# First half step of a fused attention and FFN kernel: its product in two stages, another order of issue, and products of zeros at four places

## The chip, the cores and the metric

The kernel runs on one core of one Trainium2 chip. The metric is the device time of one execution in microseconds, median of three runs. Engines are named as the trace names them: PE is TensorE (products), PEld its weight loads, DVE is VectorE, ACT is ScalarE, POOL is GpSimd, SP is SyncE, which here issues all transfers.

## The reference

Chunked attention with 8 memory keys (4 batches, 8 heads, 768 positions, head size 64), and behind it a two-layer network on the 3072x512 result, in float32:

```python
for c in range(S // 32):
    k_full = concat(mem_k, k[:, :, max(0, 32*c - 16) : 32*c + 32 + 8])   # v_full likewise
    scores = q_c @ k_full.T / sqrt(64)
    a = exp(scores - max(scores)); a = a / (sum(a) + 1e-09)
    out[:, :, c] = a @ v_full
x = out as 3072 x 512
h = x @ w_in                                    # 512 -> 2048
g = where(h >= 1, h, where(h <= -1, 0, (h + 1)**2 / 4))
return g @ w_out                                # 2048 -> 512
```

## The kernel before

The 3072 tokens are cut into 6 blocks of 512. A block's attention gives `xth` and `xtl`, the rounded high part of x and the rest; every large product is made of three: high by high, high by low, low by high. For each of 16 slices `fc` of the hidden width, a **hidden step** (`ps_h`) makes 12 products of x with a slice of `w_in`, ACT and DVE turn them into `gw`, `gh`, `gl`, and an **output step** (`ps_o`) makes 12 products with a slice of `w_out`, added up in two pairs of banks `a0`, `a1` over all 16 slices.

The weights come packed: 16 packets `w0` to `w15`, two slices each. A packet is decoded by one ACT scaling, three DVE steps on `f`, an ACT cast to `wr` and a DVE subtraction for the low part (`decode`).

Blocks 0 and 1 are written as generators that a hand-laid table, `FIRST`, advances one step per name; each engine runs its instructions in the order in which the steps are issued:

- `g0` to `g3`, `first_attention`: the first block's attention in four groups (two halves of the tokens by two pairs of heads). Steps: scores on PE (`ps_s`), maximum on DVE (`mx`), subtraction (`pr`), exponential on ACT, sum (`den`), its +1e-9, reciprocal (`rin`), division (`pr`), four PE transposes into a `ps_h` bank, ACT's copy (`pt`), the values on PE (`ps_x`), ACT's cast `xth`, DVE's subtraction `xtl`.
- `n0` to `n3`, `attention`: the halves of the next two blocks in the same steps, with DVE transposes; scores and values share one pair of banks, `s`, so n1's scores wait until DVE has read n0's values for `xtl`.
- `A`, `B`, `J`, `C`, `D`, `E` with a slice number, `early_step`: a hidden and an output step. A and B take one half of block 0's tokens each (256 columns), J takes all; C, D, E are the same for block 1.
- `w`: `decode`. `+`: the next transfer of the list `early`, issued by SP; each later use of one of 8 transfer semaphores waits for the transfer before it.

From block 2 on a regular loop does a hidden step and the output step of two slices before. `PLACES` names the banks of each group: g0 `s`, g1 `a0`, g2 scores and values `a1`, g3 scores `a1`, values `s` (as pairs of scores and values: `("s","s")`, `("a0","a0")`, `("a1","a1")`, `("a1","s")`).

Ahead of everything, `keep_warm(8)` issues eight bf16 products of zeros, 512 columns wide, into a `ps_h` bank. All records of the profile carry line L63, the helper `InOrder` that keeps the program's order, so tiles' names are what tells them apart.

Of the kernel before, what the change touches and what calls it, by code (L numbers as in the profile page):

```python
# [28 lines left out]

FIRST = """
    + + g0 g0 + g0 g1 g0 + g0 g1 g1 g0 g0 + g1 g0 w0 g1 g0 + g1 g1 g1 g0 w0 g1 + w0 g2 g1 w0 g1 g2 +
    w0 g2 w1 g0 w0 + g2 w1 g1 g2 + g0 g2 g2 g2 + g0 g2 w1 g3 g2 g1 w1 + A0 w2 g3 w1 g3 A1 w2 + g3 w1
    w3 g3 g2 A0 g3 g3 + A1 g3 A2 w2 g2 w4 g3 g2 A2 A0 w2 g3 A0 + g3 w3 w2 A0 w3 A0 g3 g3 + w2 B0 A1
    w3 A3 A1 B0 + A1 w3 B0 B1 w4 B0 w3 A3 A1 + B1 B0 w4 w5 B2 B1 w6 A2 w4 n0 + A2 B1 A2 w4 B1 A2 A3
    w5 A3 B2 + A3 w5 B3 w8 B2 w7 B0 w4 + B2 w5 B3 A3 w9 B2 B3 B1 w6 B3 + w5 w6 J4 w10 B3 w5 + w6 w11
    B2 w7 J4 w7 J5 + w6 w7 w12 w6 + w7 B3 J4 J5 w8 J6 w7 + J4 J5 w13 J4 w9 J5 J4 J6 w9 + J5 w15 J6
    w9 J7 J6 w14 J6 n0 w9 J5 J7 w9 w8 J7 J8 w8 J7 J7 w8 w11 J6 w8 J8 w11 J8 J9 w10 J8 w10 w11 J7 J9
    J8 w10 w11 J9 n0 w10 J10 J9 w10 n0 J9 w12 J8 J10 w12 w12 J11 J10 w12 w11 J10 J10 w13 J9 J11 w12  # L40
    w13 w14 J12 J11 n0 J11 n0 n0 J10 n0 J12 J11 n0 n0 J13 n0 n0 n0 n0 J11 w13 J13 J12 w13 J13 w14
    J12 n0 J13 w13 J12 J14 + n0 w14 n0 n0 w14 J12 w14 J14 J13 J14 w15 J14 n1 w15 w15 J15 + n1 w15
    w15 J13 J15 n1 J15 n1 J14 C0 J15 n1 J14 n1 n1 C0 n1 n1 J15 C1 n1 n1 J15 n1 C1 n1 n1 C1 C0 C1 C2
    J15 J15 C0 C1 n1 J15 J15 C0 C2 C2 C0 + n1 C2 n1 n1 C3 C2 C1 C3 C3 D0 C3 C3 C2 D0 D0 D1 D0 D0 n2
    D1 D1 D2 D1 + n2 C3 D1 D2 n2 D0 D2 n2 D2 D3 n2 D2 D1 n2 n2 D3 n2 E4 D3 n2 D3 n2 n2 n2 D2 E4 D3
    n2 E5 n2 E4 E4 E4 D3 E5 E6 E5 E5 E5 E4 E6 E6 E6 n2 E6 E7 + n2 n2 n2 n3 E7 E5 + n3 n3 E7 E8 n3 E7
    n3 n3 n3 E6 n3 E8 n3 n3 n3 E9 n3 n3 n3 E8 n3 E7 E8 E9 E8 E7 + n3 E9 E9 n3 n3 E9 E10 E8 E10 E10
    E10 E11 E10 E9 E11 E11 E11 E12 E11 E10 E12 E12 E12 E13 E12 E11 E13 E13 E13 E14 E13 E12 E14 E14
    E14 E15 E14 E13 E15 E15 E15 E15
"""  # L50
# [18 lines left out]
def attn_ffn_kernel(ctx: ExitStack, tc: tile.TileContext, first_qk, first_v, qk, vw, w, out):  # L69
# [24 lines left out]
    def two_banks(tag, name):  # L94
        return ps_2.tile([P, 2, 512], F32, name=name, tag=tag)
# [116 lines left out]
    def first_attention(g):  # L212
        half, u = divmod(g, 2)
        c0 = half * NCH // 2
        src = qk_of[0, g].rearrange("p (r n) -> p r n", r=2)
        ps = two_banks(PLACES[g][0], "ps_s")[:, :, 0:HT]
        s = ps.rearrange("p h (r t w) -> p h r t w", r=2, w=W)
        for r in range(2):
            for c in range(NCH // 2):
                t, j = divmod(c, P // CHUNK)  # L220
                for h in range(2):
                    rows, k0 = slice(h * D, (h + 1) * D), HT + c * W
                    pe.matmul(
                        s[j * CHUNK : (j + 1) * CHUNK, h, r, t],
                        src[rows, r, c * CHUNK : (c + 1) * CHUNK],
                        src[rows, r, k0 : k0 + W],
                        start=True,
                        stop=True,
                    )
# [12 lines left out]
        dve.tensor_reduce(m3, s, axis=AX.X, op=ALU.max)
        yield
        p4 = pr.rearrange("p (h n) w -> p h n w", h=2)
        dve.tensor_tensor(p4, s, m3.unsqueeze(3).to_broadcast([P, 2, n, W]), op=ALU.subtract)
        yield
        act.activation(pr, pr, AF.Exp, scale=SCALE)
        yield
        yield from normalise(pr)

        ps = ps_h.tile([P, 512], F32, name="ps_h")
        for n in range(NG // 2):
            pe.transpose(ps[:, n * P : (n + 1) * P], pr[:, 2 * n : 2 * n + 2, :], ident)
# [198 lines left out]
    def early_step(name, blk, tokens, fc):  # L452
# [9 lines left out]
        wh, wl = weights(0, fc, 0), weights(0, fc, 1)  # L462
        terms = hidden_terms(wh, wl, xh, xl)
        for i, (m, x, cc) in enumerate(terms):
            pe.matmul(hp, m[:, cc * P : (cc + 1) * P], x[:, cc], start=i == 0, stop=i == len(terms) - 1)
        yield
        if n == 0:
# [236 lines left out]
```

## Time and profile before

| | us |
|---|---|
| median of 3 runs (608.12 to 608.40) | 608.17 |
| the profiled execution | 608.17 |
| its span in the profile | 606.4 |
| PE busy | 591.0 (97%) |
| DVE busy | 325.6 (54%) |
| ACT busy | 281.2 (46%) |

The span is what the profile shows from the first to the last instruction; the rest of an execution's time lies around it. The page's strips cut the span into 40 equal slices of 15.2 us; PEclk is the granted TensorE clock in tenths of 2.4 GHz. In the rows further down a time is in us from the span's start.

### The profile page before, as it was taken

Reading aid. Unit: us, or ns where it says so; the run is one execution under the profiler, and the core shown is the slowest. Engines: PE = TensorE matmul, PEld = TensorE weight load, DVE = VectorE, ACT = ScalarE, POOL = GpSimd, SP = SyncE. Lnnn points to the kernel's source line nnn. Section 1 sums busy time; section 2 is a strip of 40 time slices with the busy share of each in tenths; the row PEclk is TensorE's granted clock in tenths of the full one; section 3 lists DMA queues with packets and bytes.
Section 4 is the critical chain, followed back from the end, with each engine's and each line's share of the span. In section 5 each row is a group of like instructions: output and inputs, shape, how many; then the busy total and the mean of one; then the engine's idle time right before and its main releaser. Section 6 shows DMA issues by size and latency. Waiting matters only on the chain.

```text
span 606.4 us, 12265 instructions
## 1 busy us (share of the span) xinstructions
PE 591.0 (97%) x5496; PEld 483.7 (80%) x5496; DVE 325.6 (54%) x466; ACT 281.2 (46%) x503; POOL 0.7 (0%) x6
## 2 busy tenths in 40 slices
PE   5889999999999999999999999999999999999996
PEld 2888888888888888888888888888888888888885
DVE  5999999987483224736424734623553632322222
ACT  2689764544444434344434434434433343533342
POOL 0000000000000000000000000000000000000000
PEclk8699999999999999999999999999999999999999
DMA  8999200433131004012201213101310000100001
GB/s 353 423 418 420 124 1 1 175 110 137 31 145 70 1 0 175 30 42 105 70 1 73 103 70 106 70 1 54 121 70 2 1 2 0 70 0 1 0 1 69
DMA packets 9845, 55.31 MB, mean 91 GB/s; under 512 B 1089, under 2 KB 1089, under 8 KB 5185
## 3 DMA queue, kind: packets, MB, share of 16 engines
q1 hardware_dynamic: 9792, 54.53, 23.2%
q8 instruction: 43, 0.70, 0.5%
q14 instruction: 10, 0.07, 0.0%
HBM read 48.23 MB, written 6.29 MB: 90 GB/s over the span
## 4 chain that ended last, share of the span: by engine, by line
PE 94%; DVE 3%; ACT 1%; DMA 1%; issue 0%; DVEq 0%; ACTq 0%
PE ps_o L63 44%; PE ps_h L63 44%; PE ps_x L63 3%; PE ps_s L63 3%; DVE f L63 1%; DMA qk<-in_first_qk_dram 1%; DVE pr L63 1%; DVE mx L63 0%; DVE den L63 0%; ACT w L63 0%; ACT gw L63 0%; DVE wr L63 0%; DVE xtl L63 0%; ACT pr L63 0%; ACT wr L63 0%
## 5 line engine op out<-in xcount | busy, mean ns | idle before, releaser
L63 PE MATMUL ps_o<-wr,gh 128*128 128x512 f32 x768 | 199.5, 396 | 0.0
L63 PE MATMUL ps_h<-xth,wr 128*128 128x512 f32 (+1 forms) x832 | 197.3, 379 | 0.0
L63 PEld LDWEIGHTS ps_h<-xth,wr 128*128 128x128 f32 x832 | 148.7, 189 | 31.9 <-DVE wr L63 0.5
L63 PEld LDWEIGHTS ps_o<-wr,gh 128*128 128x128 f32 x768 | 143.7, 188 | 32.5
L63 DVE SCALAR_TENSOR_TENSOR gw<-gw,gt 128x512 f32<-128x512 f32 (+1 forms) x104 | 67.2, 648 | 170.0 <-ACT gw L63 169.5
L63 ACT ACTIVATE gw<-ps_h 128x512 f32<-128x512 f32 (+1 forms) x104 | 58.7, 564 | 167.8 <-PE ps_h L63 167.7
L63 PE MATMUL ps_o<-wr,gl 128*128 128x512 f32 x384 | 109.0, 394 | 0.0
L63 PE MATMUL ps_h<-xtl,wr 128*128 128x512 f32 (+1 forms) x416 | 105.2, 375 | 0.0
L63 DVE TENSOR_TENSOR gl<-gw,gh 128x512 fp32r<-128x512 f32 (+1 forms) x104 | 67.4, 649 | 67.4 <-ACT gh L63 67.3
L63 ACT CAST gh<-gw 128x512 fp32r<-128x512 f32 (+1 forms) x104 | 61.1, 590 | 68.7 <-DVE gw L63 68.7
L63 PEld LDWEIGHTS ps_h<-xtl,wr 128*128 128x128 f32 x416 | 75.3, 190 | 14.1
L63 PEld LDWEIGHTS ps_o<-wr,gl 128*128 128x128 f32 x384 | 72.5, 189 | 17.2
L63 ACT ACTIVATE gw<-gw 128x512 f32<-128x512 f32 (+1 forms) x104 | 62.5, 601 | 0.0
L63 ACT ACTIVATE gt<-ps_h 128x512 f32<-128x512 f32 (+1 forms) x104 | 58.2, 559 | 0.0
L63 DVE STREAM_TRANSPOSE pt<-pr 32x512 f32<-32x512 f32 (+1 forms) x60 | 41.2, 698 | 1.3
L63 DVE SCALAR_TENSOR_TENSOR f<-w,f 128x1024 uint32<-128x1024 uint32 x32 | 38.9, 1220 | 0.4
L63 PEld LDWEIGHTS ps_x<-pt,v 64*64 64x64 f32 x1536 | 25.2, 142 | 5.5 <-issue 3.5
L63 ACT ACTIVATE pr<-pr 128x1024 f32<-128x1024 f32 (+1 forms) x14 | 13.1, 937 | 35.5 <-DVE pr L63 35.4
L63 PE MATMUL ps_x<-pt,v 64*64 64x32 f32 x1536 | 26.7, 226 | 1.6 <-ACT pt L63 1.6
L63 ACT CAST xth<-ps_x 128x512 fp32r<-128x512 f32 x24 | 13.1, 590 | 21.6 <-PE ps_x L63 21.5
L63 PEld LDWEIGHTS ps_s<-qk 64*32 64x32 f32 x1536 | 16.7, 110 | 6.4 <-issue 3.2
L63 ACT CAST wr<-f 128x1024 fp32r<-128x1024 f32 x16 | 16.8, 1050 | 9.3 <-DVE f L63 9.3
(27 smaller groups left out, 182.1 us busy)
## 6 DMA issues: line engine op xcount, KB each, us to landing
w<-in_w_dram SPq DMA_DIRECT2D x16, 1024.0 KB, 19.8
qk<-in_qk_dram SPq DMA_DIRECT2D x10, 1536.0 KB, 6.7
v<-in_vw_dram SPq DMA_DIRECT2D x10, 1024.0 KB, 5.1
out_dram<-ob SPq DMA_DIRECT2D x24, 256.0 KB, 2.0
qk<-in_first_qk_dram SPq DMA_DIRECT2D x4, 768.0 KB, 8.8
v<-in_first_v_dram SPq DMA_DIRECT2D x4, 512.0 KB, 12.8
```

The costliest lines, as they stand in the source:

```text
L63: return self.tc.keep_in_program_order(getattr(self.engine, name)(*args, **kwargs))
```

## The change

The table `FIRST` is replaced by another that advances the same generators in another order. Three things are new beside it:

- A name such as `z40x128` in the table calls `keep_warm(40, 128)`: 40 bf16 products of zeros, 128 columns wide, each with its weight load. There are four: 7 of 256 columns between the scores of g0 and g1, 40 of 128 behind g1's scores, 6 of 256 behind g0's transposes, 4 of 256 behind g1's.
- `keep_warm` writes into a bank of its own, `spare` (`ps_w`, in the pair `a1`), until g2's scores are issued, and `warm` is a constant tile.
- The step named by `APART`, A0, issues its 12 products in two stages: the eight with `xth`, a return to the table, and then the four with `xtl`.

The diff, with the table cut to its first lines:

```diff
 FIRST = """
-    + + g0 g0 + g0 g1 g0 + g0 g1 g1 g0 g0 + g1 g0 w0 g1 g0 + g1 g1 g1 g0 w0 g1 + w0 g2 g1 w0 g1 g2 +
-    w0 g2 w1 g0 w0 + g2 w1 g1 g2 + g0 g2 g2 g2 + g0 g2 w1 g3 g2 g1 w1 + A0 w2 g3 w1 g3 A1 w2 + g3 w1
+    + + g0 z7x256 g0 + g0 g1 z40x128 g0 + g0 g1 g0 g0 g1 + g0 g1 w0 g1 g0 z6x256 + g1 g1 g1 g0 w0 g1
+    z4x256 + w0 g2 g1 w0 g0 g2 + w0 g2 w1 g1 w0 + g2 w1 g0 g2 + g1 g0 A0 g2 g2 + g1 g2 g3 w1 A0 g3 +
...
 """
+
+APART = "A0"
...
         ps = two_banks(PLACES[g][0], "ps_s")[:, :, 0:HT]
+        if g == 2:
+            both["s2"] = True
...
         for i, (m, x, cc) in enumerate(terms):
+            if name == APART and i == 2 * NP:
+                yield
             pe.matmul(hp, m[:, cc * P : (cc + 1) * P], x[:, cc], start=i == 0, stop=i == len(terms) - 1)
...
-    def keep_warm(n):
-
-        ps = ps_h.tile([P, 512], F32, name="ps_h")
+    def keep_warm(n, cols):
+
+        ps = ps_h.tile([P, 512], F32, name="ps_h") if "s2" in both else spare
         for _ in range(n):
-            pe.matmul(ps, warm[:, 0:P], warm, start=True, stop=True)
+            pe.matmul(ps[:, 0:cols], warm[:, 0:P], warm[:, 0:cols], start=True, stop=True)
...
-    warm = gpool.tile([P, DM], BF16, name="warm", tag="gw")
+    warm = const.tile([P, DM], BF16, name="warm")
+    spare = two_banks("a1", "ps_w")[:, 0]
     dve.memset(warm, 0.0)
-    keep_warm(8)
+    keep_warm(8, DM)
...
+        if name[0] == "z":
+            keep_warm(*map(int, name[1:].split("x")))
+            continue
```

What it moves is read from the order of the built programs. First PE, from g2's scores (`qk_2`) to the first hidden steps (`wr_280` before and `wr_337` after are packet w0's decoded slices, the other one in these rows w1's; `pr_274` and `pr_331` hold g2's and g3's probabilities). Before:

```order
L63 MATMUL ps_s<-qk_2_189 32x64 x32
L63 MATMUL ps_x<-pt_127,v_130 64x32 x64
L63 MATMUL ps_h<-ident,pr_274 128x128 x4
L63 MATMUL ps_s<-qk_3_278 32x64 x32
L63 MATMUL ps_h<-xth,wr_280 128x256 x8
L63 MATMUL ps_h<-xtl,wr_280 128x256 x4
```

After:

```order
L66 MATMUL ps_s<-qk_2_242 32x64 x32
L66 MATMUL ps_x<-pt_134,v_137 64x32 x64
L66 MATMUL ps_h<-xth,wr_337 128x256 x8
L66 MATMUL ps_s<-qk_3_335 32x64 x32
L66 MATMUL ps_h<-xtl,wr_337 128x256 x4
L66 MATMUL ps_h<-ident,pr_331 128x128 x4
```

A0's eight products with `xth` now stand ahead of g3's scores, its four with `xtl` behind them, and g2's transposes come last.

Then DVE in the same place, from the sum of g2 (`f` of `w_203` or `w_260` is packet w1). Before:

```order
L63 TENSOR_REDUCE den<-pr_274 128x8
L63 TENSOR_SCALAR den<-den 128x8
L63 RECIPROCAL rin<-den 128x8
L63 TENSOR_TENSOR pr_274<-pr_274,rin 128x512
L63 TENSOR_TENSOR xtl<-ps_x,xth 128x2x256
L63 SCALAR_TENSOR_TENSOR f<-w_203,f 128x1024
L63 TENSOR_TENSOR xtl<-ps_x,xth 128x2x256
L63 SCALAR_TENSOR_TENSOR f<-w_203,f 128x1024
L63 TENSOR_REDUCE mx<-ps_s 128x8
```

After:

```order
L66 TENSOR_REDUCE den<-pr_331 128x8
L66 TENSOR_TENSOR xtl<-ps_x,xth 128x2x256
L66 TENSOR_SCALAR den<-den 128x8
L66 RECIPROCAL rin<-den 128x8
L66 TENSOR_TENSOR xtl<-ps_x,xth 128x2x256
L66 TENSOR_TENSOR pr_331<-pr_331,rin 128x512
L66 SCALAR_TENSOR_TENSOR f<-w_260,f 128x1024
L66 TENSOR_REDUCE mx<-ps_s 128x8
L66 TENSOR_TENSOR pr_331<-ps_s,mx 128x512
```

Both `xtl` moved ahead of g2's division, and one of the two steps of w1 moved behind g3's maximum.

Third, PE from n0's values (`ps_x<-pt,v`) to n1's scores (`ps_s<-qk`). Before:

```order
L63 MATMUL ps_x<-pt,v 64x32 x64
L63 MATMUL ps_h<-xth,wr_1220 128x512 x8
L63 MATMUL ps_h<-xtl,wr_1220 128x512 x4
L63 MATMUL ps_o<-wr_1220,gh 128x512 x8
L63 MATMUL ps_o<-wr_1220,gl 128x512 x4
L63 MATMUL ps_s<-qk 32x64 x64
L63 MATMUL ps_h<-xth,wr_1315 128x512 x8
```

After:

```order
L66 MATMUL ps_h<-xth,wr_1251 128x512 x8
L66 MATMUL ps_h<-xtl,wr_1251 128x512 x4
L66 MATMUL ps_x<-pt,v 64x32 x64
L66 MATMUL ps_o<-wr_1251,gh 128x512 x8
L66 MATMUL ps_o<-wr_1251,gl 128x512 x4
L66 MATMUL ps_s<-qk 32x64 x64
L66 MATMUL ps_h<-xth,wr_1394 128x512 x8
```

The hidden step that stood between the values and the scores now stands ahead of the values.

Last, DVE around the two `xtl` of n0. Before:

```order
L63 STREAM_TRANSPOSE pt<-pr 32x512 x4
L63 SCALAR_TENSOR_TENSOR f<-w_847,f 128x1024
L63 SCALAR_TENSOR_TENSOR gw<-gw,gt 128x512 x2
L63 SCALAR_TENSOR_TENSOR f<-w_854,f 128x1024
L63 TENSOR_TENSOR wr_1220<-f,wr_1220 128x1024
L63 TENSOR_TENSOR gl<-gw,gh 128x512
L63 SCALAR_TENSOR_TENSOR f<-w_854,f 128x1024
L63 TENSOR_TENSOR xtl<-ps_x,xth 128x4x2x64 x2
```

After:

```order
L66 STREAM_TRANSPOSE pt<-pr 32x512 x3
L66 TENSOR_SCALAR f<-w_951 128x1024
L66 SCALAR_TENSOR_TENSOR gw<-gw,gt 128x512
L66 TENSOR_SCALAR f<-w_939 128x1024
L66 SCALAR_TENSOR_TENSOR f<-w_939,f 128x1024
L66 TENSOR_TENSOR gl<-gw,gh 128x512
L66 SCALAR_TENSOR_TENSOR f<-w_939,f 128x1024
L66 TENSOR_TENSOR xtl<-ps_x,xth 128x4x2x64 x2
```

The first step of packet 15 (`w_951`) moved ahead of these `xtl`; over the whole stretch from packet w0's first step to them DVE has 125 instructions before and 127 after, the other one being a `gl`.

## Rows read from the trace of the kernel before

**Rows 1.** Stretches: length, each engine's busy us (instructions), clock, DMA share, GB/s.
```profile
0.00:111.90 111.90, 101.15 (x1176) 82.73 (x1176) 104.02 (x143) 74.15 (x122) 0.70 (x6) 0.92 0.60 245
...
111.90:601.76 489.86, 489.85 (x4321) 401.01 (x4320) 220.52 (x322) 206.66 (x380) 0.00 (x0) 1.00 0.15 55
...
13.42:109.94 96.52, 92.59 (x1028) 78.06 (x1029) 95.55 (x127) 68.79 (x116) 0.00 (x0) 0.93 0.57 236
```

**Rows 2.** Waits of PE: waiting line, waited for, us in total, times, longest.
```profile
PE ps_h L63 <- DVE pr L63: 6.6, 3, 4.1
```

**Rows 3.** Stretches of one us, columns as in rows 1: the clock.
```profile
9.00:10.00 1.00, 0.00 (x0) 0.00 (x0) 0.93 (x3) 0.00 (x0) 0.00 (x0) 0.58 1.00 422
...
18.00:19.00 1.00, 1.00 (x50) 1.00 (x44) 1.00 (x2) 1.00 (x2) 0.00 (x0) 0.50 1.00 408
...
26.00:27.00 1.00, 1.00 (x10) 1.00 (x9) 1.00 (x3) 1.00 (x2) 0.00 (x0) 0.89 1.07 434
```

**Rows 4.** Timeline of PE and PEld: start, us, engine, operation, count, idle before.
```profile
1.59 0.15 PEld L63 LDWEIGHTS <-warm 128*128 128x128 bf16 x1 [0.28 <-issue]
...
6.89 0.86 PE L63 MATMUL ps_s<-qk 64*32 64x64 f32 x64 [0.83 <-DMA qk<-in_first_qk_dram]
11.88 1.09 PE L63 MATMUL ps_h<-ident,pr 128*128 128x128 f32 x4 [4.13 <-DVE pr L63]
...
15.08 1.19 PE L63 MATMUL ps_s<-qk 64*32 64x64 f32 x64 [0.35 <-DMA qk<-in_first_qk_dram]
16.20 3.64 PE L63 MATMUL ps_x<-pt,v 64*64 64x32 f32 x128
...
23.72 2.08 PE L63 MATMUL ps_h<-xth,wr 128*128 128x256 f32 x8
...
26.36 1.11 PE L63 MATMUL ps_h<-xth,wr 128*128 128x256 f32 x8
...
29.05 1.22 PE L63 MATMUL ps_h<-xth,wr 128*128 128x256 f32 x8
...
30.59 0.60 PE L63 MATMUL ps_h<-ident,pr 128*128 128x128 f32 x4
32.77 1.14 PE L63 MATMUL ps_x<-pt,v 64*64 64x32 f32 x64 [1.58 <-ACT pt L63]
33.83 1.20 PE L63 MATMUL ps_o<-wr,gh 128*128 128x512 f32 x4
```

**Rows 5.** Timeline of DVE: the divisions of g0 and g3, g2's maximum and sum, w1.
```profile
11.04 0.69 DVE L63 TENSOR_TENSOR pr<-pr,rin 128x512 f32<-128x512 f32 x1
...
16.54 0.68 DVE L63 TENSOR_REDUCE mx<-ps_s 128x8 f32<-128x512 f32 x1
...
19.60 0.68 DVE L63 TENSOR_REDUCE den<-pr 128x8 f32<-128x512 f32 x1
...
23.70 1.22 DVE L63 SCALAR_TENSOR_TENSOR f<-w,f 128x1024 uint32<-128x1024 uint32 x1
24.83 0.68 DVE L63 TENSOR_REDUCE mx<-ps_s 128x8 f32<-128x512 f32 x1
...
29.05 0.69 DVE L63 TENSOR_TENSOR pr<-pr,rin 128x512 f32<-128x512 f32 x1
```

**Rows 6.** Timeline of ACT: the two casts of g0 and g1, a packet's scaling, a cast `gh`.
```profile
19.24 1.25 ACT L63 CAST xth<-ps_x 128x512 fp32r<-128x512 f32 x2
...
30.22 1.18 ACT L63 ACTIVATE w<-w 128x1024 f32<-128x1024 f32 x1
...
32.56 0.46 ACT L63 CAST gh<-gw 128x256 fp32r<-128x256 f32 x1
```

**Rows 7.** Timeline of DVE ahead of n1's scores.
```profile
96.00 0.25 DVE L63 RECIPROCAL rin<-den 128x16 f32<-128x16 f32 x1
96.29 1.22 DVE L63 TENSOR_TENSOR pr<-pr,rin 128x1024 f32<-128x1024 f32 x1
...
108.65 1.28 DVE L63 TENSOR_TENSOR xtl<-ps_x,xth 128x512 fp32r<-128x512 f32 x2
```

More of the change, by code (lines that the diff above doesn't have):

```diff
@@ L32 @@
 FIRST = """
-    + + g0 g0 + g0 g1 g0 + g0 g1 g1 g0 g0 + g1 g0 w0 g1 g0 + g1 g1 g1 g0 w0 g1 + w0 g2 g1 w0 g1 g2 +
-    w0 g2 w1 g0 w0 + g2 w1 g1 g2 + g0 g2 g2 g2 + g0 g2 w1 g3 g2 g1 w1 + A0 w2 g3 w1 g3 A1 w2 + g3 w1
-    w3 g3 g2 A0 g3 g3 + A1 g3 A2 w2 g2 w4 g3 g2 A2 A0 w2 g3 A0 + g3 w3 w2 A0 w3 A0 g3 g3 + w2 B0 A1
-    w3 A3 A1 B0 + A1 w3 B0 B1 w4 B0 w3 A3 A1 + B1 B0 w4 w5 B2 B1 w6 A2 w4 n0 + A2 B1 A2 w4 B1 A2 A3
-    w5 A3 B2 + A3 w5 B3 w8 B2 w7 B0 w4 + B2 w5 B3 A3 w9 B2 B3 B1 w6 B3 + w5 w6 J4 w10 B3 w5 + w6 w11
@@ L38 @@
[L38 to L47, printed above, removed]
@@ L48 @@
-    E10 E11 E10 E9 E11 E11 E11 E12 E11 E10 E12 E12 E12 E13 E12 E11 E13 E13 E13 E14 E13 E12 E14 E14
-    E14 E15 E14 E13 E15 E15 E15 E15
+    + + g0 z7x256 g0 + g0 g1 z40x128 g0 + g0 g1 g0 g0 g1 + g0 g1 w0 g1 g0 z6x256 + g1 g1 g1 g0 w0 g1
+    z4x256 + w0 g2 g1 w0 g0 g2 + w0 g2 w1 g1 w0 + g2 w1 g0 g2 + g1 g0 A0 g2 g2 + g1 g2 g3 w1 A0 g3 +
+    g2 g3 A0 w1 g3 A1 g2 g3 w1 + g3 g3 g3 w2 g2 A0 w1 A1 g3 + g2 w2 A2 A0 g2 g3 A0 w4 w2 g3 A2 w2 A0
+    g3 + w3 g3 A2 B0 w2 A1 w3 A2 w3 A1 + n0 B0 w2 B1 B0 A1 + B0 w4 A1 w5 B0 w3 B1 B2 A2 + w3 w4 A3
@@ new lines @@
+    B2 B1 w3 B1 w6 B3 + B2 B1 A3 w4 A2 B3 A3 w5 w4 + B0 w5 A3 B2 J4 w7 w4 w8 + B2 w6 w9 A3 B3 B1 w6
+    B3 J4 + w5 J5 w10 B3 J4 w5 w6 + B2 J4 w5 w11 A3 J4 J5 + w7 w7 B3 w12 w7 J6 w6 + J5 w13 w6 J5 n0
+    w7 + J4 w14 J5 w7 J6 + J7 w8 w15 J6 w8 J6 J6 J5 J7 w8 w9 w8 J7 w9 J8 J7 w9 w8 w9 J6 J8 J7 w10 w9
+    J9 w10 w11 w10 J7 J9 n0 J8 n0 J9 w11 J9 J10 J8 J9 w10 J8 n0 J8 J10 w10 n0 n0 w12 J10 J11 w11 J10
+    n0 w11 J10 J9 J11 w11 w12 J12 J11 w13 J11 w12 J11 w12 J10 w13 J12 w12 J12 J13 w13 J12 J12 w13 n0
@@ new lines @@
+    n0 J11 J13 n0 w13 n0 J14 n0 n0 w15 J13 n0 w14 J13 w14 J14 J13 J12 + n0 w14 n0 n0 w14 w14 n1 J14
+    J15 w15 J14 + J14 w15 J13 n1 w15 J15 n1 w15 C0 n1 J15 J14 n1 C0 J15 C0 n1 n1 C0 J15 n1 C1 C0 n1
+    J15 C1 n1 n1 n1 n1 C2 n1 C1 n1 J15 J15 C1 C2 C1 J15 J15 C2 C3 + n1 C2 n1 n1 C0 C3 C2 D0 C3 C3 C3
+    C1 D0 D0 D1 D0 D0 C2 D1 D1 D2 D1 D1 C3 D2 D2 D3 D2 D2 D0 D3 D3 E4 D3 D3 D1 E4 E5 E4 E4 E4 D2 E5
+    E6 E5 E5 E5 D3 n2 E6 E4 E6 + n2 E6 E6 n2 E7 n2 n2 E5 E7 n2 n2 n2 E7 E8 n2 E7 n2 E7 n2 n2 E6 E8
@@ L50 @@
+    n2 n2 E8 E8 n2 E8 E9 + n2 n2 n2 E7 E9 E9 E9 E10 E9 E8 E10 E10 E10 E11 E10 E9 E11 E11 E11 n3 E11
+    E10 + n3 n3 E12 n3 n3 n3 n3 E11 n3 E12 n3 n3 n3 E13 n3 n3 n3 E12 n3 E13 E12 E13 E14 + n3 E12 E13
+    n3 n3 E13 E12 E14 E14 E14 E15 E14 E13 E15 E15 E15 E15
 """
+APART = "A0"
 LAST = 2
```

## The prediction

> **What bounds the kernel now.** The table of stretches comes first: TensorE (PE) is busy for 101.15 of the first 111.90 us, idle for 10.75, and idle for 0.01 of the next 489.86 [rows 1], to 601.76, where only the last store is left. So after the first ramp the kernel is a queue of products without a gap, and a change in the ramp is worth as much as it brings that queue forward. TensorE's waits name the ramp's largest loss: 6.6 us behind VectorE's (DVE's) `pr` in three waits [rows 2]. The granted clock is the second loss: 0.58 in 9 to 10 us, 0.50 until it comes back in 26 to 27 [rows 3], that is 1.2 instead of 2.4 GHz, after TensorE had idled from 7.75 (6.89+0.86 [rows 4]). Third view: DVE is busy 95.55 of the 96.52 us from 13.42 to 109.94 [rows 1]. Through the ramp DVE, not TensorE, has no slack; TensorE can work ahead of it only as far as the order allows.
>
> The profiled execution took 608.17 us, its span 606.4; the 1.77 outside stay, and 608.17 is also the median of the runs shown. I call faster or slower what moves by over 0.2%, 1.22 us, about what a measurement of this kernel can tell from no change.
>
> **Where both orders meet.** The scores of n1 (64 products on `ps_s`, 111.90 before) are the place to compare at: behind them stand 3168 products in either program, the same number of each shape. Before, TensorE runs from there to 601.76 with no wait [rows 1]. If the order after has none there either, the end moves by as much as the start of these scores. That start is the later of two: TensorE's own arrival, and DVE's release, since the scores overwrite the bank from which n0's two `xtl` are still read.
>
> **The order's part: TensorE's arrival.** DVE's work is unmoved up to the sum `den` of g2 at 19.60 [rows 5]; g2's scores cannot start before their load, and started at 15.08 [rows 4]. From 19.60 I set each instruction in the new order behind its engine and its inputs, with the lengths of the rows. ACT's two casts `xth` run 19.24 to 20.49 [rows 6], so A0's first eight products start near 19.9 instead of 23.72. At the high clock twelve 256-column products took 30.59-29.05=1.54, 0.12 to 0.13 each [rows 4], so eight end near 20.9, and g3's scores (0.86, the row at 6.89) near 21.8. DVE now does `xtl` of g0, `den`, `rin`, `xtl` of g1, the division of g2, one step of w1: 0.6+0.2+0.2+0.6+0.6+1.1=3.4 after 20.2, so the maximum of g3 stands at 23.5 (24.83 before). From there to its division are 0.7+0.6+1.1+0.7+0.2+0.2=3.6 of DVE's steps, the 1.1 being a step of w1 (23.70 to 24.83): 27.1 (29.05 before [rows 5]). Before, g3's values came 3.7 after the division (32.77), behind ACT's copy of `pt`; ahead of that copy ACT now has a `gh` (0.46) where it had the scaling of a packet (1.18 [rows 6]): 3.0 to 3.1, so 30.2. The first output product follows 1.06 later as before (32.77 to 33.83), near 31.3 [rows 4], behind the same 36 hidden products in both orders. TensorE leads by 2.5 us there. One new wait of 0.4 follows near 41 by the same walk, where a hidden step waits for ACT's read of its bank; I come to an arrival at n1's scores of 111.90-2.5+0.4, about 109.8, at best 109.4.
>
> **DVE's release.** Before, DVE ends the second `xtl` of n0 at 109.93 [rows 7] and TensorE comes 1.97 later, since a hidden step and an output step lie between n0's values and n1's scores. The new order has only the output step there, so this slack goes. And DVE has two instructions more ahead of that `xtl`: one `gl` and the first step of weight packet 15. An instruction that needs nothing of the one before starts 0.09 before that one's recorded end (23.70+1.22 to 24.83 [rows 5]), so 512 elements, 0.68 long, move DVE on by 0.6: both by 1.2. One that reads what its neighbour wrote starts 0.04 after the end (96.00+0.25 to 96.29 [rows 7]), so such a pair costs 0.13 more; I count 21 of them before (the transposes left aside), 17 after: -0.5. Release: 109.93+1.2-0.5=110.63, and 0.15 from DVE's end to TensorE's start, as at the first transposes (11.04+0.69=11.73 to 11.88 [rows 4, 5]): **110.8**. It is later than the arrival, so it decides: TensorE waits about 1.0 for DVE, and of the lead of 2.5 us 111.90-110.8=**1.1** are left. DVE's chain hands on every delay one to one; the count of pairs and ACT's coming in time leave about 0.4 on either side.
>
> **The zeros' part.** Product by product they cost TensorE, not DVE; all stand where it waited: 7 between the scores of g0 and g1 (idle 0.83), 40 ahead of g0's transposes (4.13), 6 ahead of g1's, 4 ahead of g2's scores (0.35) [rows 4]. They cost nothing while g2's scores end before DVE wants their maximum, 16.54 [rows 5]. The trace has no small bf16 product. Lower bound by columns: the first zeros, 512 wide, came 0.43 apart (a load of 0.15, idle for 0.28 before it [rows 4]), the pace of the low clock, so 128 take 0.107 low and half, 0.054, high, 256 twice that. Upper bound: the weight load ahead of each took 0.15 [rows 4]; nothing shows that it overlaps a short product, so 0.15 for 128 columns, and 0.21 for 256 at the low clock. Nearest row: the 256-column fp32r products, 0.12 with their loads; I take 0.12 for both. From 7.75: 40x0.12=4.8, transposes 0.60 (30.59 [rows 4]), 0.7, transposes 0.6, 0.5: 14.95, ahead of g2's load; its scores end near 15.95, 0.6 to spare. At the lower bound TensorE waits as before. At the upper one, all at the low clock: 7.75+6.0+1.09+1.28+1.09+0.85+1.19=19.25, 2.7 too late.
>
> The Trainium skill ("TensorE: Matmul & The Clock Gate", section LDWEIGHTS (loading the stationary operand)) has a weight load go by its columns alone, columns over 1.2 ns. By that, an estimate, a zero of 128 columns costs 0.107 and the 40 of them 4.3; rival (2) below could then not come about, and the sum would stay.
>
> **What the clock is worth.** Between 12 and 26 us the low clock costs TensorE some 4 us: values 3.64 for 128 against 2x1.14, transposes 1.09 against 0.60, first hidden products 2.08 against 1.22 [rows 4]. But DVE bounds this stretch, so a high clock gives nearly nothing beyond the 1.1 that the order already gives; a low one costs only where TensorE comes late for DVE.
>
> Sum: 606.4-1.1=605.3 of span, 608.17-1.1=**607.1 us**; with 0.4 either way 606.7 to 607.5.
>
> **Rivals.** (1) *The clock falls among the zeros or is low behind them.* For it: it fell at 9.2 once 1.4 us were idle, and TensorE busy with small fp32 work from 15.08 to 19.84 did not bring it back: 0.50 throughout [rows 3, 4]. If it falls at 9.2 again, the last 15 of the 40 zeros take 1.6, over by 10.8; then 11.6+1.09+1.28+1.09+0.85+1.19=17.1 for g2's scores, 0.55 later than DVE wants them: gain 0.55, **607.6**. Against: TensorE does not stand still at 7.75 any more. The Trainium skill's page on TensorE ("TensorE: Matmul & The Clock Gate", Part 4: PE-mode transpose) says that transposes do not count as busy for the clock gate; by that the zeros must hold it alone, which makes this rival likelier. The trace neither shows nor excludes it: during the transposes at 11.88 the clock is low, but it had fallen before them.
>
> (2) *Slower: zeros at their upper price in front of g2's scores.* One mechanism: short products do not hide their weight loads, the clock stays low, and g2's scores end at 19.25. DVE stands at its maximum of g2 for 2.7 us, everything behind it moves: -1.1+2.7=+1.6, **609.8**. It decides from 1.1 of lateness on, scores ending at 17.65: that needs 0.11 per zero of 128 columns and the low clock from the start. For it: no row shows such a product. Against: TensorE's loads overlap products wherever rows show both.
>
> (3) *Faster: DVE is not the last at n1's scores.* Had its chain some 1 us to give, TensorE's arrival at 109.4 to 109.8 would decide: gain 2.1 to 2.5, **605.9**. Against: DVE is full and has more to do than before, not less.
>
> (4) *The lead is lost on the way.* New waits near 24 to 26 (1.6 us for `pt` of g2) let the clock fall for some microseconds: two groups of twelve hidden products at 2.64 (23.72 to 26.36) instead of 1.54, 2.2 later, so TensorE arrives at 111.6 to 112.0 and decides: gain 0.1, **608.1**. For it: the fall at 9.2 followed such an idle stretch; against: dense wide products lie around the waits, and from 26.36 on these kept the clock up before [rows 3, 4].
>
> **How the numbers follow.** Forecast 0.58, (1) 0.18, (2) 0.08, (3) 0.11, (4) 0.05. Of the forecast's own spread about two fifths lies under 606.95, the bound of faster: 0.24; with (3) 0.35. Slower: (2), and little else, 0.09. Within 0.2%: 0.56. The range takes in forecast, (1), (4) and the near part of (3): **606.2 to 608.4**.
>
> **What would show it.** Right: g2's maximum on DVE near 16.5; A0's first product near 19.9; first output product near 31.3; one wait of about 1 us of TensorE for DVE's `xtl` ahead of n1's scores, these at 110.8, and no TensorE wait after; clock high or not without much effect on these. Wrong: n1's scores without a wait for DVE (then the gain is above 2); g2's maximum later than 16.5 by more than it gains; waits of TensorE behind 112 us, where I assume none.

## The result

| kernel | median us | range, runs | ratio to before, 95% interval |
|---|---|---|---|
| before | 608.12 | 607.97 to 608.40, 5 | 1 |
| changed | 611.16 | 611.08 to 611.26, 5 | 1.0049 (1.0036 to 1.0062) |

The changed kernel is slower by 3.0 us, 0.5%. The prediction was 607.1 with a range up to 608.4: wrong in the size and in the sign. The profiled execution has a span of 609.4 us (606.4 before).

First the stretches of the changed kernel, which answer to [rows 1]: length, busy time of PE, PEld, DVE, ACT and GpSimd with instruction counts, granted clock, DMA share, GB/s.

```profile
0.00:114.63 114.63, 104.43 (x1233) 85.26 (x1234) 103.50 (x143) 73.70 (x122) 0.70 (x6) 0.97 0.58 237
114.63:604.76 490.13, 490.13 (x4320) 400.90 (x4320) 220.89 (x322) 206.52 (x380) 0.00 (x0) 1.00 0.15 55
...
5.00:22.00 17.00, 10.15 (x378) 8.62 (x381) 13.89 (x25) 6.53 (x9) 0.00 (x0) 1.00 1.02 420
22.00:28.80 6.80, 6.80 (x107) 5.80 (x100) 5.10 (x7) 2.26 (x6) 0.00 (x0) 0.50 1.03 425
```

The scores of n1, the meeting point, stand at 114.63 and not at 111.90 or at the predicted 110.8. Behind them TensorE has no gap, as predicted, but the stretch is 490.13 long and not 489.86. So 2.73 of the 3.0 us are lost in the ramp and 0.27 behind it. The granted clock was high (1.00, 2.4 GHz) from 5 to 22 us, where before it fell at 9.2 [rows 3], and low (0.50, 1.2 GHz) from there to 28.8. The zeros did this: in the new order without them, further down, it fell at 9.15 again.

The waits of PE in the changed kernel (waiting line, waited for, us in total, times, longest) answer to [rows 2], and below them are those of DVE from 13.5 to 115 us, where the same view of the kernel before lists none:

```profile
PE ps_x L66 <- issue: 4.0, 2, 3.8
PE ps_s L66 <- issue: 1.8, 2, 1.4
PE ps_h L66 <- DVE pr L66: 1.7, 2, 1.1
...
DVE xtl L66 <- ACT xth L66: 2.2, 1, 2.2
DVE gw L66 <- ACT gw L66: 0.9, 2, 0.6
DVE mx L66 <- PE ps_s L66: 0.4, 1, 0.4
```

The wait for `pr` fell from 6.6 to 1.7 us. In its place stand 5.8 us of "issue" on PE: idle time in which the engine waits for nothing that the profile shows. The kernel before has none of it on PE. The timeline of PE tells where (start, length, operation, count, idle before); compare it with [rows 4]:

```profile
7.72 2.41 PE L66 MATMUL ps_w<-warm 128*128 128x128 bf16 x40
...
15.25 0.98 PE L66 MATMUL ps_s<-qk 64*32 64x64 f32 x64 [1.02 <-DMA qk<-in_first_qk_dram]
16.16 1.47 PE L66 MATMUL ps_x<-pt,v 64*64 64x32 f32 x84
21.47 1.03 PE L66 MATMUL ps_x<-pt,v 64*64 64x32 f32 x44 [3.83 <-issue]
22.43 2.39 PE L66 MATMUL ps_h<-xth,wr 128*128 128x256 f32 x8
...
33.31 0.78 PE L66 MATMUL ps_x<-pt,v 64*64 64x32 f32 x38
34.26 0.59 PE L66 MATMUL ps_x<-pt,v 64*64 64x32 f32 x26 [0.17 <-issue]
34.78 1.20 PE L66 MATMUL ps_o<-wr,gh 128*128 128x512 f32 x4
...
37.80 1.07 PE L66 MATMUL ps_s<-qk 64*32 64x64 f32 x84
40.27 0.69 PE L66 MATMUL ps_s<-qk 64*32 64x64 f32 x44 [1.40 <-issue]
...
114.63 1.64 PE L66 MATMUL ps_s<-qk 64*32 64x64 f32 x128 [0.41 <-issue]
```

TensorE stops in the middle of a run of equal products: after 84 of the 128 value products of g0 and g1, and again after 84 of n0's 128 score products. (The trace has two records for each of these small fp32 products, 128 for the program's 64, each with a weight load; counts of products here are counts of records.) The profile shows no wait for a semaphore there, and inputs and bank are the same as for the product ahead. The 3.83 us then run through ScalarE and VectorE (timelines of ACT and DVE; compare [rows 5, 6]):

```profile
22.54 0.59 ACT L66 CAST xth<-ps_x 128x512 fp32r<-128x512 f32 x1 [2.78 <-PE ps_x L66]
...
16.27 0.69 DVE L66 TENSOR_REDUCE mx<-ps_s 128x8 f32<-128x512 f32 x1
...
23.15 0.69 DVE L66 TENSOR_TENSOR xtl<-ps_x,xth 128x512 fp32r<-128x512 f32 x1 [2.15 <-ACT xth L66]
...
25.98 0.69 DVE L66 TENSOR_REDUCE mx<-ps_s 128x8 f32<-128x512 f32 x1 [0.40 <-PE ps_s L66]
...
113.25 1.28 DVE L66 TENSOR_TENSOR xtl<-ps_x,xth 128x512 fp32r<-128x512 f32 x2
```

DVE, which had no slack, idles 2.15 us for the second half of these values, and its chain hands that on to n0's second `xtl`, which ends at 113.25+1.28=114.53. n1's scores start 0.10 later.

### The profile page after: what moved, and what is told of

Same layout as the page of the kernel before. It is cut to its first block, busy times and chain, and to the rows that moved or that the text cites. A ratio compares the mean times of both kernels' runs of the same rounds, so it can differ in the third digit from the quotient of the medians.

```text
span 609.4 us, 12376 instructions
## 1 busy us (share of the span) xinstructions
PE 594.6 (98%) x5553; PEld 486.2 (80%) x5553; DVE 325.4 (53%) x466; ACT 280.6 (46%) x503; POOL 0.7 (0%) x6
## 4 chain that ended last, share of the span: by engine, by line
PE 95%; DMA 2%; issue 1%; ACT 1%; SPq 0%; DVE 0%; DVEq 0%; ACTq 0%
PE ps_h L66 44%; PE ps_o L66 44%; PE ps_x L66 4%; PE ps_s L66 3%; DMA qk<-in_first_qk_dram 2%; SPq L66 0%; ACT w L66 0%; ACT wr L66 0%; ACT gw L66 0%; DVE ob L66 0%; ACT gt L66 0%; ACT pr L66 0%; ACT pt L66 0%; ACT ob L66 0%; DVEq L711 0%
## 5 line engine op out<-in xcount | busy, mean ns | idle before, releaser
L66 PE MATMUL ps_s<-qk 64*32 64x64 f32 x1536 | 19.2, 229 | 3.2 <-issue 1.8
```

The costliest lines, as they stand in the source:

```text
L66: return self.tc.keep_in_program_order(getattr(self.engine, name)(*args, **kwargs))
```

## Where the idle "issue" time sits

The page of either kernel has one DMA queue that the prediction never looked at (queue, kind, packets, MB, share):

```profile
q8 instruction: 43, 0.70, 0.5%
```

43 packets of 16384 bytes. TensorE's records in the trace (matmuls, weight loads, semaphore instructions) number some 11,000, and 43 times 256 is 11,008, which suggests that this queue feeds TensorE's instruction stream, 256 instructions to a packet. I numbered the records in order of time, counting from 0, and looked where the idle stretches of the changed kernel fall: ahead of the 705th record (3.83), the 1217th (0.17) and the 1473rd (1.40). 1217-705=512 and 1473-1217=256. They stand at multiples of 256 from each other, at borders of blocks, and each ends just behind a packet of that queue. The table is worked out from the trace: when the first record behind a border ran, and when the next packet of that queue moved.

| border (record) | before: entered | next packet | changed: entered | next packet |
|---|---|---|---|---|
| 449 | 16.54 | 19.93 to 20.94 | 15.56 | 19.04 to 20.03 |
| 705 | 22.66 | 26.21 to 27.29 | 21.47 | 25.47 to 26.55 |
| 961 | 28.68 | 33.55 to 34.59 | 28.65 | 31.67 to 32.74 |
| 1217 | 38.36 | 40.53 to 41.59 | 34.26 | 37.87 to 38.94 |
| 1473 | 43.53 | 47.24 to 48.35 | 40.27 | 44.05 to 45.15 |

In the changed kernel a packet starts 3.0 to 4.0 us after TensorE enters the block ahead of it (2.2 to 4.9 in the kernel before), takes 1.0 to 1.1, and where TensorE waits for it, it goes on 1.3 to 1.5 us after the packet's end (20.03 to 21.47, 32.74 to 34.26, 38.94 to 40.27). Together that is some 6 us for a block. 128 value products with their weight loads are 256 instructions and run in 2.3 us. So **in the loaded stretch that the table covers, up to some 45 us, TensorE gets a block of 256 instructions only every 6 us or so, however short they are.** The kernel before lived close to this: its 705th record ran 1.7 us after its packet had landed, its 961st 1.4 after. The 57 products of zeros are 114 instructions. They move every border 114 records back in the work: the 705th record, in g3's scores before, now falls into g1's values.

## The experiments

The theory (supply): what is lost hangs on how many instructions TensorE has run by when, and on where the borders fall. The rivals: the new order, the zeros' own length, the clock that they hold.

**The count, not the columns.** The zeros are made 32 columns wide, their number stays.

```
-    + + g0 z7x256 g0 + g0 g1 z40x128 g0 + ... z6x256 + ... z4x256
+    + + g0 z7x32 g0 + g0 g1 z40x32 g0 + ... z6x32 + ... z4x32
```

> The changed kernel with its 57 products of zeros 32 columns wide in place of 128 and 256: as many instructions, a fifth of the columns. Theory (supply): the count decides, not the columns; the idle stretch inside g1's values stands at the same product (the 705th record), ends near 21.4 and the time is 610.8 to 611.8. Rival (the zeros' own length, or the full clock that they hold, brings the stop): the clock falls as in the kernel before, the stretch is gone, 606.5 to 608.2.

Measured: 611.21 us, 1.0048 (1.0035 to 1.0061). PE's timeline:

```profile
16.25 2.56 PE L66 MATMUL ps_x<-pt,v 64*64 64x32 f32 x84
21.28 1.49 PE L66 MATMUL ps_x<-pt,v 64*64 64x32 f32 x44 [2.47 <-issue]
```

The stop is after the same 84 products, though the clock had fallen at 11.85, and it ends at the same time. It is shorter only because the values ran slower ahead of it. The time is that of the changed kernel, so columns and clock are out.

**The same instructions elsewhere.** In the kernel before, the first 8 products of zeros become 64 narrow ones, in the first 5 us.

```
-    keep_warm(8)
+    keep_warm(64)
-            pe.matmul(ps, warm[:, 0:P], warm, start=True, stop=True)
+            pe.matmul(ps[:, 0:64], warm[:, 0:P], warm[:, 0:64], start=True, stop=True)
```

> The kernel before, in which the first 8 products of zeros (512 columns) are 64 of 64 columns: the same columns, 56 products or 112 instructions more, all in the first 5 us, where TensorE waits for the first load anyway. Theory (supply): the border of the 705th record moves back by 112 records, from g3's scores into g1's values; TensorE idles 2 to 3.5 us there, near 19 to 21.4, ten microseconds and more behind the added instructions: 609.2 to 611. Rival (what an instruction costs, it costs where it stands): no change, 607.9 to 608.4.

Measured: 610.29 us, 1.0037 (1.0025 to 1.0050).

```profile
16.20 2.56 PE L63 MATMUL ps_x<-pt,v 64*64 64x32 f32 x86
21.33 1.48 PE L63 MATMUL ps_x<-pt,v 64*64 64x32 f32 x42 [2.56 <-issue]
```

The old order, no zeros at the four places, 112 instructions in idle time at the start: 2.2 us lost 15 us later, after 86 products, as the count says. DVE idles 1.96 for `xtl` here.

**The zeros in the old order**, with the changed kernel's `keep_warm`, its bank and its constant tile.

```
-    + + g0 g0 + g0 g1 g0 + ... w0 g1 g0 + ... w0 g1 + w0 g2
+    + + g0 z7x256 g0 + g0 g1 z40x128 g0 + ... w0 g1 g0 z6x256 + ... w0 g1 z4x256 + w0 g2
```

> The kernel before with the 57 products of zeros at the same four places; its order of work unchanged, A0 in one stage. Theory (supply): the border of the block (705th record) moves back by 114 records, from g3's scores into g1's values, after some 86 of their 128 pairs; it is crossed near 21.4, so TensorE idles about 3.3 us there with no releaser named; VectorE has its second half of g1's values later by about 2.5 and the whole ramp moves by 1 to 3: 609.2 to 611. Rival (order): no such idle stretch, the zeros lie in idle time: 607.8 to 608.4.

Measured: 611.37 us, 1.0054 (1.0042 to 1.0066), 0.4 over the expected range.

```profile
16.02 1.47 PE L67 MATMUL ps_x<-pt,v 64*64 64x32 f32 x85
21.41 1.49 PE L67 MATMUL ps_x<-pt,v 64*64 64x32 f32 x43 [3.91 <-issue]
```

The zeros alone cost as much as the whole change, and the new order is not needed for it. (The run with the order alone, below, loses 2.5 us without any of them.)

**More instructions.** The first 8 products become 32, the 40 become 80, with the same columns.

```
-    keep_warm(8, DM)
+    keep_warm(32, DM // 4)
-    ... z40x128 ...
+    ... z80x64 ...
```

> The changed kernel with more products of zeros and the same columns: 32 of 128 columns in place of the first 8 of 512, and 80 of 64 in place of 40 of 128, 64 products or 128 instructions more. Theory (supply): the block's border moves 128 records back in the work, to g1's values after some 20 of their 128 pairs; the block ahead of it is now entered at about 13.0, as soon as it is there, so this border is crossed near 19 and not 21.47, and A0's first products come near 21.3 and not 22.43: about 1 us less than the changed kernel, 609.5 to 610.7, though there are more instructions. Rival (each product of zeros costs by itself): 3.0 us more for 57 make 3.4 more for 64: 614.5.

Measured: 610.93 us, 1.0045 (1.0033 to 1.0057).

```profile
17.02 0.54 PE L66 MATMUL ps_x<-pt,v 64*64 64x32 f32 x21
18.61 2.06 PE L66 MATMUL ps_x<-pt,v 64*64 64x32 f32 x107 [1.05 <-issue]
```

The border sits after 21 products (20 expected) and is passed at 18.61; A0's first products stand at 20.60, 1.8 us earlier than in the changed kernel. The next border then stops g3's scores after 12 products for 1.64 us, and the gain is gone: 0.2, within the spread of the runs, and not 1; the expected range is missed by 0.2. A fixed cost for each product (614.5) is excluded. This run also shows the pace of the supply best: TensorE enters its blocks at 11.82, 18.61, 25.01, 31.40, 37.91 and 43.71, each 5.8 to 6.8 us behind the one ahead, and stands idle at four of these six borders.

**Fewer instructions.** 19 products of 512 columns for the 57.

```
-    ... z7x256 ... z40x128 ... z6x256 ... z4x256
+    ... z4x512 ... z10x512 ... z3x512 ... z2x512
```

> The changed kernel with about the same columns of zeros in 19 products of 512 in place of 57 of 128 and 256: 76 instructions less. Theory (supply): the border of the 705th record moves 76 records on, to just ahead of the last pairs of g1's values; the block behind it is entered about 6 us after the 449th record, which is now crossed near 16.1: near 22.1, so A0's first products stand at 22.2 in place of 22.43, the idle stretch is still 3.5 us, and little is won: 610.2 to 611.2. Rival (a cost for each product of zeros, 3.0 us for 57): 1.0 for 19, 609.1.

Measured: 615.49 us, 1.0114 (1.0094 to 1.0133). Both expectations missed.

```profile
16.04 2.05 PE L66 MATMUL ps_x<-pt,v 64*64 64x32 f32 x122
21.68 0.31 PE L66 MATMUL ps_x<-pt,v 64*64 64x32 f32 x6 [3.60 <-issue]
...
36.92 1.43 PE L66 MATMUL ps_s<-qk 64*32 64x64 f32 x122
42.60 0.32 PE L66 MATMUL ps_s<-qk 64*32 64x64 f32 x6 [4.25 <-issue]
```

The first stop came as expected, ahead of the last 6 pairs and 3.60 long. I had not followed the border of the 1473rd record: it moved to the end of n0's scores, whose 256 instructions then made up nearly one whole block, and TensorE stood for 4.25 us. Fewer instructions, 4.3 us slower: it is the place of the borders that counts. (The two stops stand two records short of the multiples of 256 here; the trace can miss a few records.)

**The order alone.** No zeros at the four places; order and two stages of A0 stay.

```
-    + + g0 z7x256 g0 + g0 g1 z40x128 g0 + ... w0 g1 g0 z6x256 + ... w0 g1 z4x256 + w0 g2
+    + + g0 g0 + g0 g1 g0 + ... w0 g1 g0 + ... w0 g1 + w0 g2
```

> The changed kernel without the 57 products of zeros at four places; the new order and the two stages of A0 stay. Theory (supply): TensorE's instructions come in blocks of 256, each a transfer of 16384 bytes, and a block can be entered only about 6 us after the one ahead of it was entered (21.47 after 15.56 in the changed kernel, where the 705th record is the first of a block). Without the 114 instructions of the zeros that border moves 114 records on in the work, out of g1's values into g3's scores, and is reached about when its block is there: no idle stretch over 0.5 us inside g1's values, A0's first products near 20, and the lead of the order stays: 607.0, between 606.5 and 608.2. Rival (order): the new order itself asks for more than it can have; idle of 3 to 4 us inside g1's values as before, 610.5 to 611.5.

Measured: 610.64 us (609.86 to 612.59), 1.0045 (1.0034 to 1.0057). Half of the theory came true, its time did not. The time is the one that the rival gives, but not for the rival's reason, a stop inside g1's values:

```profile
16.23 3.64 PE L66 MATMUL ps_x<-pt,v 64*64 64x32 f32 x128
19.80 2.43 PE L66 MATMUL ps_h<-xth,wr 128*128 128x256 f32 x8
...
35.30 1.68 PE L66 MATMUL ps_s<-qk 64*32 64x64 f32 x128
...
41.81 0.96 PE L66 MATMUL ps_o<-wr,gh 128*128 128x512 f32 x3 [2.97 <-issue]
```

The values run without a stop and A0 starts at 19.80. But the lead brings n0's 256 short instructions 7 us forward (42.60 before), and the block behind them is not there: TensorE idles 2.97 us, the granted clock is 0.50 from 43.3 to 46.7, and DVE idles 3.7 in all. (The profiled execution is one of the slower ones here, 611.74.)

**The order with n0's scores later.** They move from ahead of the hidden step B1 to behind B3.

```
-    ... w3 A1 + n0 B0 w2 B1 B0 A1 + ... B1 w6 B3 + B2
+    ... w3 A1 + B0 w2 B1 B0 A1 + ... B1 w6 B3 n0 + B2
```

> The new order without the zeros, and n0's 128 score products (256 instructions, run in 1.7 us) moved from ahead of the hidden step B1 to behind the hidden step B3; the loads as they were. Theory (supply): the block from the 1217th record then holds hidden and output steps, 24 instructions in 1.44 us, lasts over 6 us, and the idle stretch of 2.97 us ahead of the 1473rd record goes (under 0.5 us); a wait of up to 1.6 us for the gl of A1 comes near 37, which n0's scores covered; the clock stays up past 43: 606.8 to 608.4. Rival (the loss comes with any lead over VectorE, given back in another wait): 609.5 to 611.

Measured: 608.28 us (11 runs), 1.0003 (0.9995 to 1.0012). The stop is gone, as the theory says; n1's scores follow DVE (first row DVE, second PE):

```profile
110.07 1.28 DVE L50 TENSOR_TENSOR xtl<-ps_x,xth 128x512 fp32r<-128x512 f32 x2
...
111.45 1.47 PE L50 MATMUL ps_s<-qk 64*32 64x64 f32 x128
```

Moving one step took 2.4 us out. What is left of the order's gain is 0.45 us at the meeting point, and behind it 490.23 in place of 489.86.

**The changed kernel with n0's scores later.** The same move, zeros kept.

> The changed kernel with all its zeros, and n0's score products moved behind the hidden step B3 as in the run before without zeros. It takes the second border's loss alone from the changed kernel. Theory: the idle stretch of 3.83 us inside g1's values stays, the one of 1.40 at the 1473rd record goes; VectorE's idle time ahead of the second xtl of n0 falls from 3.45 us to 2.55 (2.15 and 0.40), so that xtl ends near 113.6 and n1's scores stand at 113.7: 610.2, between 609.7 and 610.7. With the run before (608.28) that leaves some 2 us for the 57 products of zeros. Rival (the losses do not add): as the changed kernel, 611.0 to 611.4, or as without zeros, 608.3.

Measured: 610.99 us, 1.0041 (1.0027 to 1.0055): above the expected range, at the lower edge of the rival's.

```profile
16.21 1.47 PE L50 MATMUL ps_x<-pt,v 64*64 64x32 f32 x84
21.79 1.49 PE L50 MATMUL ps_x<-pt,v 64*64 64x32 f32 x44 [4.10 <-issue]
```

The stop at the 1473rd record went, but in this execution the first was 0.27 longer and DVE's idle time 3.15 (2.79 and 0.36) for 3.45. The time is the changed kernel's but for 0.2 us, which these runs can't tell from nothing. So one stop is enough for the loss, and here the losses of the two stops do not add.

**The loads held.** Why does a packet of instructions need 3.5 us to start? From 5 to 22 us the DMA share is 1.02. In the order alone, the loads behind packet 5 are held until about 39, by the name `h6` in the table; v of n0 is loaded later, and two transfers are issued behind `h6`.

```
-    ... A1 + n0 B0 w2 B1 B0 A1 + B0 w4 A1 w5 B0 w3 ...
+    ... A1 n0 B0 w2 B1 B0 A1 B0 w4 A1 w5 B0 h6 + + w3 ...
+        if name[0] == "h":
+            i = int(name[1:])
+            raw[i] = const.tile([P, 2 * n2], U32, name=f"w_{i}", tag=f"w_{i}")
+            pool.tensor_copy(raw[i][0:1, 0:1], both["gl"][0:1, 0:1].bitcast(U32))
...
-        (load_w, 2), (load_w, 3), (load_w, 4), (load_qk, 1, 0), (load_v, 1, 0),
+        (load_w, 2), (load_w, 3), (load_w, 4), (load_qk, 1, 0),
...
-    early += [(load_w, i) for i in range(5, NPW)]
+    early += [(load_w, i) for i in range(5, NPW)] + [(load_v, 1, 0)]
```

> The new order without the zeros (as in the run with the order only), and the loads held once: the load of v of n0 goes behind the 16 weight packets, and the load of packet 6 waits, through a copy of one word on GpSimd, for VectorE's gl of B0, at about 39. So no load runs from about 36 to 40, where TensorE enters the block of its 1217th record (35.6) and ran out of instructions for 2.97 us before the 1473rd (41.81). Theory (the block's transfer stands behind the loads): its packet comes within 1.5 us of the crossing and not 3.7 later, the idle stretch shrinks to under 0.5 us, the clock does not fall at 43: 606.5 to 608.2. Rival (a fixed spacing of 6 us between blocks, whatever the loads do): packet and idle stretch as in the run with the order only, 609.9 to 611.5.

Measured: 616.77 us, 1.0136 (1.0118 to 1.0155). The mechanism shows, the time is far off. The 1217th record ran at 35.07, the next packet came at 36.21 (1.14 later, 3.68 with the loads running) and the 1473rd record at 38.52, with 0.22 idle in place of 2.97. What the two DMA queues moved meanwhile, first in the order alone from 36 to 39.2 us, where the loads fill the DMA engines and no instruction packet moves, then with the loads held from 35 to 36.2 and from 36.2 to 37.2; last TensorE at the border:

```profile
q1 hardware_dynamic: 185, 1.34, 100.5%
...
q1 hardware_dynamic: 4, 0.00, 0.2%
...
q8 instruction: 1, 0.02, 6.0%
...
38.52 0.96 PE L50 MATMUL ps_o<-wr,gh 128*128 128x512 f32 x3 [0.22 <-issue]
```

But the loads stood still for some 11 us (34.8 to 46.1), nearly 6 of them through the copy on GpSimd, and ScalarE then waited for packet 6:

```profile
39.25 5.86 POOL L50 COPY w<-gl 1x1 uint32<-1x1 uint32 x1 [37.95 <-DVE gl L50]
...
50.05 1.14 ACT L50 ACTIVATE w<-w 128x1024 f32<-128x1024 f32 x1 [7.37 <-DMA w<-in_w_dram]
```

**The same hold on the kernel before**, by the same lines but behind the gl of A1, as a control:

> The kernel before with the same hold of the loads (v of n0 behind the weights, packet 6 after the gl of A1, at about 38.6). A control: the kernel before has no idle stretch at a block's border there, so the theory expects no difference, 607.8 to 608.5. Rival (holding the loads helps or harms by itself, through weights that come later): 606.5, or over 609.

Measured: 616.64 us, 1.0121 (1.0094 to 1.0148). No control, since the copy took 5.33 us here too and ScalarE waited 6.56 for packet 6; it says only that the ramp cannot spare its loads that long (8.4 us slower).

**A shorter hold**, ended by VectorE:

```
-            pool.tensor_copy(raw[i][0:1, 0:1], both["gl"][0:1, 0:1].bitcast(U32))
+            dve.memset(raw[i][0:1, 0:1], 0)
```

> As the run with held loads, but the hold ends by a memset of one word on VectorE behind the gl of B0, at about 39.3: in that run the copy on GpSimd took 5.86 us (39.25 to 45.11), so the loads stood still for 12 us and ScalarE waited 7.37 us for packet 6. Theory: the block behind the 1473rd record still comes in time (idle under 0.5 us in place of 2.97), packet 6 lands near 42, and no new wait of over 1 us arises: 606.6 to 608.0, 2.5 to 4 less than with the order only. Rival (holding the loads at all costs as much as it brings): 609.5 or more.

Measured: 612.03 us, 1.0061 (1.0047 to 1.0074). Again the packet comes at once (1217th record 35.74, packet 36.62, 1473rd record 38.96, idle under 0.2), and again ScalarE waits, now 2.66 us:

```profile
45.94 1.13 ACT L50 ACTIVATE w<-w 128x1024 f32<-128x1024 f32 x1 [2.66 <-DMA w<-in_w_dram]
```

The rival's time is right: holding the loads costs at least what it brings. The fixed spacing of 6 us, however, is excluded by both runs: the two blocks behind the 1217th and the 1473rd record were entered 3.2 and 3.5 us apart while no load ran.

**Smaller load packets.** Every weight load in four.

```
-        sp.dma_start(raw[i][:, a:b], w[i, :, a // 2 : b // 2].bitcast(U32))
+        for a in range(0, 2 * n2, n2 // 2):
+            b = a + n2 // 2
+            sp.dma_start(raw[i][:, a:b], w[i, :, a // 2 : b // 2].bitcast(U32))
```

> The changed kernel with every weight load cut in four, so that its packets are 2 KB and not 8 KB; bytes and order stay. Theory A (a block's packet waits for the packets that already stand queued at its DMA engine, a fixed number of them): the packet comes 1 to 2.5 us after a border is crossed where weights load, and not 3.5 to 4.0; the idle stretch in g1's values shrinks from 3.83 to 1.5 to 3, the one at the 1473rd record goes; 608.5 to 610.3. Theory B (the wait is by bytes or by time): 3.5 to 4.0 as in the changed kernel, idle 3.8 and 1.4, 610.8 to 611.8.

Measured: 613.43 us, 1.0084 (1.0054 to 1.0113), outside both ranges. The instruction packets started 3.6, 2.3, 3.5, 4.2 and 2.9 us after the borders 449 to 1473: no clear change, so theory A is not borne out. g2's load came later here (TensorE waits 2.77 for it, and g2's scores start at 16.93 in place of 15.25), which would explain most of the 2.3 us on top; that is argued and not tested. That the loads delay the instruction packets is shown by the two runs with held loads; by what rule the two share the DMA engines stays open.

## Why the prediction was wrong

- **Meeting point: right**, but for 0.27 us of tail. In [rows 1] the tail was 489.86; with the new order it is 490.13 (changed kernel) and 490.23 (n0 later), in one profiled execution each.
- **DVE's release decides: right, and its size nearly.** In the new orders n1's scores start 0.10 us after the second `xtl` of n0 ends: 114.53 to 114.63, 115.10 to 115.20 (order alone), 111.35 to 111.45 (n0 later), 114.42 to 114.52 (n0 later, with the zeros), 115.61 to 115.71 (short hold). The profile calls part of that "issue", but the equal 0.10 speaks for the release. Predicted 110.8. Take DVE's new idle time away and the changed kernel has 114.63-3.45=111.18, the order with n0 later 111.45-0.45=111.00, with the zeros 114.52-3.15=111.37, and the order alone 115.20-3.70=111.50. The sum of DVE's steps was 0.2 to 0.7 short.
- **"They cost nothing while g2's scores end before DVE wants their maximum": the step that failed.** The sum has the zeros at nothing under a condition that came true, and they cost all the same: g2's maximum stood at 16.27 (16.5 predicted, 16.54 before [rows 5]). As work they were even cheaper than the prediction took them: 0.056 us each for 128 columns and 0.11 for 256, start to start in the timeline, its lower bounds and not the 0.12 taken. The estimate of 0.107 for 128 columns after the Trainium skill ("TensorE: Matmul & The Clock Gate", LDWEIGHTS (loading the stationary operand)) was twice too high here: the records of these weight loads are 0.098 long, but they overlap one another. What the zeros cost is their count: 114 instructions ahead of a border. The sum has no term for the supply of instructions. In this execution DVE lost 2.15 and 0.40 us behind the stop at the 705th record and 0.90 in waits near 46 to 49 (`gw`), behind the stop at the 1473rd: 3.45 where the sum has nothing.
- **TensorE's arrival: wrong by the same omission.** I set each product behind its engine and its inputs and took for granted that it is there to be issued. The new order alone fails by this too: without the zeros it loses 2.5 us at another border, and adding them to it changes the time by no more than the runs can tell (610.64 and 611.16). A0's first product was to come at 19.9; it came at 22.43, but at 19.80 without the zeros. The first output product was to come at 31.3 and came at 34.78, without the zeros at 32.29. In the order alone the lead meets the border of the 1473rd record and is lost there. Two of the prediction's sums are 0.1 off (DVE's 3.4 and 3.6 should be 3.3 and 3.5); nothing hangs on it, and the steps themselves were right: in the order alone g3's maximum stands at 23.37 (23.5 predicted) and its division at 27.20 (27.1).
- **The clock: right that it is worth little.** With the zeros 32 columns wide it fell at 11.85 and not at 22, and the time was the same (611.21 and 611.16).
- **Rivals.** (1) The clock did not fall among the zeros; it was low behind them, from 22 to 28.8, after the first stop. (2) Slower, as it says, but not by the zeros' price in columns and loads: the direction is right and the mechanism is not. (3) DVE was last. (4) The lead was lost on the way, as it says, but not for `pt`, and the kernel lost 3 us and did not gain 0.1.
- **The order's own gain of 1.1: too large.** With the stop at n0 removed it is 608.28, no measurable change: 0.45 at the meeting point less 0.37 in the tail.

The sum closes: span predicted 605.3, measured 609.4. Of the 4.1 us, 3.45 are DVE's new idle time, 0.38 its steps and 0.27 the tail.

What [rows 4] could have shown: 128 products with 128 weight loads in 3.64 us, next to an instruction queue with 43 packets and a DMA share of 1.0. The Trainium skill has the mechanism ("Runtime: NRT & Kernel Launch", Instruction fetch mechanics): instructions come in blocks of 16 KiB, 256 each, by a DMA queue of the engine's own, and crossing a border is "mostly hidden". The size of the blocks agrees with the 43 packets here; the hiding does not, where loads fill the DMA engines: 3.83 us at one border.

Not settled: the two stages of A0 were not tried by themselves; how the DMA engines choose between loads and instructions; and why the tail is 0.3 us longer in the new orders. How much each stop costs by itself was not measured either. No version here beats the kernel before; the nearest is the new order without zeros and with n0's scores later, 608.28.

## What to carry to other kernels

Count an engine's instructions as well as its time: where loads fill the DMA engines, a block of 256 TensorE instructions took some 6 us to arrive, so 128 short products with their weight loads, 2.3 us of work, should stand beside long ones: here, moving n0's scores behind longer steps took out a stop of 2.97 us. Idle "issue" time in the middle of equal products is the sign; number the records and see whether the stops lie a multiple of 256 apart. Filler products are not free for standing in idle time, even far ahead: they move every border behind them. Nor is a smaller number of them safe (19 wide ones cost more here than 57, and 64 more narrow ones cost nothing more): look where the borders go.

## What the runs showed of the hardware

- Products of zeros 32 columns wide, each with a weight load of 128 columns, came 0.025 us apart at the high clock (40 in 1.17 us), 128 wide 0.056 (40 in 2.41 us).
- An instruction packet started 2.0 to 4.9 us, mostly 3 to 4, after a border (449 to 1473) was crossed with the loads running, and 0.9 to 1.2 us with them held.
- A GpSimd copy of one word took 5.86 us beside a busy VectorE (39.25 to 45.11; VectorE's last instruction ended at 45.07), and 5.33 in the control. Spans on GpSimd are rough in the profile, but the loads that waited for this copy moved again only at 46.1.
